# Attention and two MLPs on one core: Q and K as whole rows, V in four transfers, smaller array tiles for attention, and a planner that counts eight transfers

## The chip, the cores and the metric

The kernel runs on one core of one Trainium2 chip. The metric is the device time of one execution in microseconds (us), lower is better. Three executions of the kernel before took 1086.65, 1087.54 and 1088.17 us; their median, 1087.54 us, is its time.

## The reference

Chunked attention (chunks of 32 queries, 16 keys to the left, 8 to the right, 8 memory keys; so 64 keys for a chunk) over 4 batches, 8 heads, 768 positions and 64 dimensions, then two MLPs over the 3072 tokens that come out:

```python
for c in range(nc):                       # chunk 32, left 16, right 8, n_mem 8
    k_full = np.concatenate([mem_k, k_ctx], axis=2)
    v_full = np.concatenate([mem_v, v_ctx], axis=2)
    scores = scale * np.matmul(q_c, k_full.transpose(0, 1, 3, 2))
    scores = scores - np.max(scores, axis=-1, keepdims=True)
    a = np.exp(scores)
    a = a / (np.sum(a, axis=-1, keepdims=True) + 1e-09)
    out[:, :, c_start:c_end] = np.matmul(a, v_full)
h = x @ w_in                              # 512 -> 2048
x = (np.maximum(h, 0) + np.log1p(np.exp(-np.abs(h)))) @ w_out
h = x @ w_in2
out = (np.maximum(h, 0) + alpha * np.minimum(h, 0)) @ w_out2
```

The weights come as 64-bit floats; the kernel turns them into 32-bit ones itself.

## The kernel before

**Stages.** The 3072 tokens are six blocks of 512 (`NB`), and a block is four attention tiles of 128 queries (`TB`), so there are 24 tiles, 0 to 23. The first MLP runs in 96 steps. A step is one slice of 128 hidden units for one block: `pe_h` (12 matmuls of 128x512, tile `ps_hh`, called *h* below), softplus and a split into a high and a low part on ACT and DVE, then `pe_out` (12 matmuls, tile `ps_o`, called *o*). `SEGMENTS` (line 49) gives the order: block 0 with slices 0 to 3, block 1 with 0 to 3, block 0 with 4 to 7, block 1 with 4 to 7, and so on, so that the weights may come in while the steps run. Steps 0 to 3 need tiles 0 to 3, and steps 4 to 7, the first of block 1, need tiles 4 to 7. The second MLP (`quad`, `second`, tile `ps_q`) follows; the change leaves its arithmetic as it is.

**A tile of attention.** `load_q`, `load_k`, `load_v` fetch it. `a_mem` copies the memory keys on POOL. `a_scores` (tile `ps_s`) does Q times K on PE; `a_max` and `a_shift` or `a_bias` run on DVE, the exponential on ACT, `a_sum`, `a_norm`, `a_share` on DVE (four shares on POOL). `a_transpose` (`ps_t`) turns the result on PE, `a_turned` copies it to `pt` on ACT, `a_values` (`ps_x`) multiplies by V on PE, `a_high` on ACT and `a_low` on DVE write the split `x`.

**Loads.** All of them are issued on SP, in program order. A Q load takes only half of the row (the other half is zeros), so tiles 0 to 7 have two Q loads of 128 KB and one K load of 320 KB; from tile 8 on it is four Q loads of 64 KB and one of 320 KB. V is six transfers for every tile. Each transfer takes one of eight completion semaphores in turn, so a transfer is issued only when the eighth before it has landed.

**Weights.** A half slice of weights is one `raw` load of 512 KB and, on DVE, five operations (`magnitude`, `clamp`, `convert`: tile `word`), then a cast on ACT and a subtraction on DVE (`wsplit`). There are three `raw` rooms.

**The planner.** `Plan` (lines 87 to 182) takes pieces with an engine, an assumed length, a due time, what they wait for and what rooms they take, and writes out one order for each engine; `schedule` (line 921) states the pieces. The table `O` (line 84) shifts the due times. Where the planner sees PE idle in the first 90 us of its own time, it puts matmuls on zeros ahead of the piece (`keep_busy`, tile operand `zero`), so many as its idle time holds.

Of the kernel before, what the change touches and what calls it, by code (L numbers as in the profile page):

```python
# [16 lines left out]
P = 128  # L17
# [17 lines left out]
KEYS = (0, NMEM + CHUNK, NMEM + 2 * CHUNK, KN - KW)  # L35
BIG = 3.0e38
# [47 lines left out]
O = {'km': 86.2, 's': 61.12, 'm': -43.08, 'c': -48.65, 'e': 42.58, 'n': -133.53, 'r': -44.0, 'w': -59.36, 't': 2.28, 'pt': -87.92, 'v': 6.67, 'xh': -71.45, 'xl': 6.28, 'first': 47.53, 'gap': -183.71, 'second': 20.97, 'gap2': -27.69, 'raw': 41.75, 'ab': -85.86, 'cl': -61.09, 'ca': 10.82, 'cb': 74.39, 'cc': -95.76, 'wh': -29.12, 'wl': -22.45, 'odd': 97.94, 'sp': 116.5, 'hi': 37.44, 'lo': 2.59, 'out': 17.61, 'wait': 0.05, 'sloads': 24.5, 'km0': 68.55, 'km1': 28.97, 's0': -25.87, 's1': 2.3, 'm0': -192.19, 'm1': -112.61, 'c0': -31.95, 'c1': -25.21, 'e0': -51.53, 'e1': -16.47, 'n0': -131.79, 'n1': 72.42, 'r0': -17.47, 'r1': -5.18, 'w0': 52.91, 'w1': -43.08, 't0': -1.99, 't1': 39.24, 'pt0': -100.96, 'pt1': 70.29, 'v0': 21.52, 'v1': 14.34, 'xh0': -72.64, 'xh1': 5.24, 'xl0': 133.53, 'xl1': -30.69, 'by0': -46.78, 'by1': 30.48, 'va': -0.63, 'vb': 176.94, 'vc': -46.03, 'vd': 155.73, 'ra': -58.02, 'rb': 154.89, 'rc': 130.18, 'wld': 105.54, 'dra': -108.27, 'ca0': 58.14, 'ca1': -5.43}  # L84


class Plan:
# [18 lines left out]
    def run(self):  # L106
# [10 lines left out]
        while left:  # L117
            able, first = [], 1e9
            for name, since in ready.items():
                engine, us, due, _, _, take, _, _ = left[name]  # L120
                t = max(since, free.get(engine, 0.0) if engine else 0.0, now)
                if engine == "SP":
                    t = max(t, free.get("DMA", 0.0) - 4.0)
                for r in set(take):
                    short = take.count(r) - rooms[r]
                    if short > 0:
                        later = sorted(u for u, g in back if g == r)
                        t = max(t, later[short - 1] + self.LAG if len(later) >= short else 1e9)
                able.append((t, due, name, engine))
# [28 lines left out]
            if engine == "PE":  # L158
# [3 lines left out]
                if t < 90.0 and t - free.get("PE", 0.0) > 0.5:  # L162
                    self.idle[name] = (max(free.get("PE", 0.0), came), t)
# [14 lines left out]
            for a in then.get(name, ()):  # L178
                wants[a] -= 1
                if not wants[a]:  # L180
                    ready[a] = max(done[b] for b in left[a][4]) + self.LAG
# [4 lines left out]
def attention_mlp_mlp_kernel(ctx: ExitStack, tc, qk, v, w1, w2, consts, out):  # L186
# [15 lines left out]
    ps_a = ctx.enter_context(room_pool("ps_a", 2, bass.MemoryType.PSUM))  # L202
    early = ctx.enter_context(ExitStack())
    apool = early.enter_context(room_pool("a", 1))
# [111 lines left out]
    raw_q, q_t, k_t, v_t, st, s_room = {}, {}, {}, {}, {}, {}  # L316
    pt = [tpool.tile([P, NPAIR, 2, D], F32, tag=tag, name="pt") for tag in ("tb", "tl")]
    both = gpool.tile([P, 2, NPAIR, 2, D], F32, tag="g", name="pt2")
    pt2 = [both[:, u] for u in range(2)]

    def pt_of(t):
        return pt2 if t < TB and t % 2 else pt

    q_late = apool.tile([P, 2, 4 * NPAIR, CHUNK], F32, tag="qt", name="qt", bufs=1)

    def others(q, eng):

        for e in range(2):
            half = q[e * D:(e + 1) * D].rearrange("p c (n e) k -> p c n e k", e=2)
            for c in range(2):  # L330
                eng.memset(half[:, c, :, 1 - e], 0.0)

    def room_qk(t):
        if t < 2 * TB:
            room = wpool.tile([P, 4 * DM], F32, tag="w", name="qk0")
            raw_q[t] = room[:, :QN // 2]
            k_t[t] = room[:, QN:QN + NPAIR * KN].rearrange("p (g k) -> p g k", k=KN)
        else:
            q_t[t] = q_late
            k_t[t] = apool.tile([P, NPAIR * KN], F32, tag="kt", name="kt", bufs=1).rearrange("p (g k) -> p g k", k=KN)  # L340

    def own(q, e):

        return q[e * D:(e + 1) * D].rearrange("p c (n e) k -> p c n e k", e=2)[:, :, :, e]

    def load_q(t, e, c=None):
        part = slice(e * D, (e + 1) * D)
        rows = qk[t][part, :QN].rearrange("p (n e k) -> p n e k", e=2, k=D)[:, :, e]
        if c is None:
            sp.dma_start(out=raw_q[t][part].rearrange("p (n k) -> p n k", k=D), in_=rows)  # L350
        else:
            sp.dma_start(out=own(q_t[t], e)[:, c], in_=rows[:, :, c * CHUNK:(c + 1) * CHUNK])
# [12 lines left out]
    def load_v(t):  # L365
        for u, to, at, n in (
            (0, 0, MEM0, NMEM), (0, NMEM, 0, KW - NMEM), (0, KW, CHUNK, KW),
            (1, 0, 0, KW), (1, KW, SW - KW + NMEM, KW - NMEM), (1, 2 * KW - NMEM, MEM0 - D, NMEM),
        ):
            part = slice(u * DM, (u + 1) * DM)  # L370
            sp.dma_start(out=v_t[t][to:to + n, part], in_=v[t][at:at + n, part])

    score_ps, turned, x_ps, part_of = {}, {}, {}, {}

    def no_corners():

        for to in (pt, pt2):
            for c in range(2):
                for u in range(2):
                    dve.memset(to[u][c * D:(c + 1) * D, :, :, (1 - c) * CHUNK:(2 - c) * CHUNK], 0.0)  # L380
# [5 lines left out]

    def a_scores(t):

        ps = score_ps[t] = (ps_acc.tile([P, NPAIR, 2, KW], F32, tag="acc", name="ps_s") if t < TB
                            else ps_a.tile([P, NPAIR, 2, KW], F32, tag="pa", name="ps_s"))  # L390
        keep_busy(("s", t), ps.rearrange("p g u k -> p (g u k)"))
        if t < 2 * TB:
            q = raw_q[t].rearrange("p (n k) -> p n k", k=D)
            for g in range(NPAIR):
                for j in range(NC):
                    u, c = divmod(j, 2)
                    for e in range(2):
                        rows, at = slice(e * D, (e + 1) * D), c * D + e * CHUNK
                        pe.matmul(
                            ps[at:at + CHUNK, g, u, :], lhsT=q[rows, u * NPAIR + g, c * CHUNK:(c + 1) * CHUNK],  # L400
                            rhs=k_t[t][rows, g, KEYS[j]:KEYS[j] + KW], start=True, stop=True,
                        )
            return
        for g in range(NPAIR):
            for j in range(NC):
                u, c = divmod(j, 2)
                n = 2 * (u * NPAIR + g)
                pe.matmul(
                    ps[c * D:(c + 1) * D, g, u, :], lhsT=q_t[t][:, c, n:n + 2, :].rearrange("p e k -> p (e k)"),
                    rhs=k_t[t][:, g, KEYS[j]:KEYS[j] + KW], start=True, stop=True,  # L410
                )

    def a_max(t):

        ps, i = score_ps[t], t % TPB
        s = s_room[t][:, :SLOTS * KW] if t < 2 * TB else apool.tile([P, SLOTS * KW], F32, tag="s", name="s_sb")
        st[t] = (s.rearrange("p (g u k) -> p g u k", u=2, k=KW), s.rearrange("p (n k) -> p n k", k=KW),
                 apool.tile([P, SLOTS, 1], F32, tag="nm", name="nm", bufs=2),
                 apool.tile([P, SLOTS, 1], F32, tag="sm", name="sm", bufs=2))
        if i == 0:  # L420
            dve.memset(ps[:D, :, 0, NMEM:NMEM + LEFT], -BIG)
        if i == TPB - 1:
            dve.memset(ps[D:, :, 1, LEFT + CHUNK:LEFT + CHUNK + RIGHT], -BIG)
        dve.tensor_reduce(out=st[t][2][:, :, 0], in_=ps.rearrange("p g u k -> p (g u) k"), axis=mybir.AxisListType.X, op=ALU.max)

    def a_shift(t):
        _, s, nm, _ = st[t]
        dve.tensor_tensor(
            out=s, in0=score_ps.pop(t).rearrange("p g u k -> p (g u) k"), in1=nm.to_broadcast([P, SLOTS, KW]), op=ALU.subtract,
        )  # L430
# [5 lines left out]
    def a_shifted_exp(t):  # L436
        _, s, nm, _ = st[t]
        x = score_ps.pop(t).rearrange("p g u k -> p (g u) k")
        for n in range(SLOTS):
            act.activation(out=s[:, n, :], in_=x[:, n, :], func=AF.Exp, bias=nm[:, n, :], scale=1.0 / float(D) ** 0.5)  # L440
# [19 lines left out]
    def a_transpose(t):  # L460
        ps = turned[t] = ps_a.tile([P, NPAIR, P], F32, tag="pa", name="ps_t")
        keep_busy(("t", t), ps.rearrange("p g k -> p (g k)"))
        for g in range(NPAIR):
            pe.transpose(ps[:, g, :], st[t][0][:, g, :, :].rearrange("p u k -> p (u k)"), ident)

    def a_turned(t):

        ps = turned.pop(t)
        for u in range(2):
            for c in range(2):  # L470
                act.copy(
                    out=pt_of(t)[u][c * D:(c + 1) * D, :, :, c * CHUNK:(c + 1) * CHUNK],
                    in_=ps[u * D:(u + 1) * D, :, c * D:(c + 1) * D].rearrange("p g (e q) -> p g e q", e=2),
                )

    def a_values(t):
        src = v_t.pop(t)
        ps = x_ps[t] = (ps_h.tile([P, NPAIR, QT], F32, tag="h", name="ps_x") if t < TB
                        else ps_a.tile([P, NPAIR, QT], F32, tag="pa", name="ps_x"))
# [715 lines left out]
```

## Time and profile before

| what | value |
|---|---|
| median of three executions | 1087.54 us (1086.65 to 1088.17) |
| the profiled execution's own time | 1092.29 us |
| its span, first to last instruction | 1090.2 us |
| mean granted TensorE clock | 0.995 of full speed |
| PE busy | 1061.8 us, 97% of the span |
| DVE busy | 705.3 us, 65% |
| ACT busy | 556.9 us, 51% |
| POOL busy | 173.0 us, 16% |
| chain that ended last | PE 92%, DMA 4%, SP's queue 2%, DVE 2% |
| read from HBM, written | 154.74 MB, 46.14 MB |

Busy time is the share in which an engine worked on something, matmuls on zeros among it. The chain follows the work that ended last back to the start, and tells for each step what it waited for. Times inside an execution are counted from the first instruction.

### The profile page before, as it was taken

The numbers are of one execution on the slowest core, as the hardware profiler recorded it, in microseconds if no ns is written. First come the engines' busy times: TensorE is split into PE (matmuls) and PEld (weight loads), VectorE is DVE, ScalarE is ACT, GpSimd is POOL, SyncE is SP. The second block draws the span as 40 slices with busy tenths as digits, with TensorE's granted clock in tenths as the row PEclk, the third lists the DMA queues.
The fourth block names the chain that finished last, engine by engine and source line by source line (L and its number), as shares of the span: only waits on it lengthen the run. The fifth ranks groups of instructions, "written<-read, shape, count | busy, mean of one in ns | idle before, by whom it ended". The sixth has DMA issues, their size and how long they took to land.

```text
span 1090.2 us, 16860 instructions
## 1 busy us (share of the span) xinstructions
PE 1061.8 (97%) x6241; PEld 872.5 (80%) x6245; DVE 705.3 (65%) x1182; ACT 556.9 (51%) x988; POOL 173.0 (16%) x217
## 2 busy tenths in 40 slices
PE   5789999999999999999999999999999999999998
PEld 3568888878888888888888888888888888888886
DVE  5779978454554454464366256678766779566976
ACT  4564435455544554453244346664455755456643
POOL 1110112422322232224233400000000010000000
PEclk8999999999999999999999999999999999999999
DMA  8966674757554554554365484799875999856904
GB/s 216 203 178 190 192 188 109 180 159 178 152 156 148 167 174 125 184 156 136 106 203 189 161 300 137 274 286 323 199 284 174 322 298 261 242 217 256 373 1 77
DMA packets 173841, 214.56 MB, mean 197 GB/s; under 512 B 96064, under 2 KB 125888, under 8 KB 166848
## 3 DMA queue, kind: packets, MB, share of 16 engines
q1 hardware_dynamic: 169456, 196.59, 56.8%
q0 software_dynamic: 4032, 16.78, 8.2%
q8 instruction: 49, 0.80, 0.3%
q14 instruction: 32, 0.26, 0.1%
q10 hardware_dynamic: 272, 0.13, 0.0%
HBM read 154.74 MB, written 46.14 MB: 184 GB/s over the span
## 4 chain that ended last, share of the span: by engine, by line
PE 92%; DMA 4%; SPq 2%; DVE 2%; issue 0%; ACT 0%; POOL 0%; DVEq 0%; ACTq 0%
PE ps_q L71 42%; PE ps_hh L71 23%; PE ps_o L71 23%; SPq L71 2%; DMA raw<-in_w_dram 2%; PE ps_x L71 2%; PE ps_s L71 2%; DMA v<-in_v_dram 1%; PE ps_t L71 1%; DVE word L71 1%; DMA qk<-in_qk_dram 1%; DVE x L71 0%; DVE wsplit L71 0%; DVE g L71 0%; ACT pt L71 0%
## 5 line engine op out<-in xcount | busy, mean ns | idle before, releaser
L71 PE MATMUL ps_o<-g,wsplit 128*128 128x512 f32 x1152 | 281.2, 393 | 1.3 <-DVE g L71 1.3
L71 PE MATMUL ps_hh<-x,wsplit 128*128 128x512 f32 x1152 | 279.4, 391 | 2.9 <-ACT x L71 1.8
L71 PEld LDWEIGHTS ps_hh<-x,wsplit 128*128 128x128 f32 x1152 | 214.7, 188 | 48.6 <-ACT x L71 2.3
L71 PEld LDWEIGHTS ps_o<-g,wsplit 128*128 128x128 f32 x1152 | 215.8, 189 | 46.6 <-DVE g L71 1.6
L71 PE MATMUL ps_q<-xop,win 128*128 128x512 f32 x1008 | 229.1, 389 | 0.0
L71 PE MATMUL ps_q<-g,wout 128*128 128x512 f32 x1008 | 229.1, 389 | 0.0
L71 PEld LDWEIGHTS ps_q<-xop,win 128*128 128x128 f32 x1008 | 189.2, 188 | 39.3
L71 PEld LDWEIGHTS ps_q<-g,wout 128*128 128x128 f32 x1008 | 189.0, 188 | 39.6 <-DVE g L71 0.2
L71 DVE TENSOR_TENSOR g<-ta,g 128x512 fp32r<-128x512 f32 x96 | 70.4, 733 | 131.1 <-ACT g L71 130.6
L71 ACT CAST g<-gb 128x512 fp32r<-128x512 f32 x168 | 100.9, 622 | 91.1 <-PE ps_q L71 66.1
L71 DVE TENSOR_TENSOR g<-gb,g 128x512 fp32r<-128x512 f32 x168 | 114.2, 687 | 37.0 <-ACT g L71 35.1
L71 ACT CAST g<-ta 128x512 fp32r<-128x512 f32 x96 | 59.6, 621 | 113.9 <-PE ps_o L71 113.7
L71 ACT ACTIVATE ta<-ps_hh 128x512 f32<-128x512 f32 x96 | 57.4, 598 | 108.9 <-PE ps_hh L71 106.6
L71 DVE SCALAR_TENSOR_TENSOR word<-raw,word 128x512 int32<-128x512 int32 x128 | 93.0, 727 | 2.7
L71 ACT ACTIVATE tp<-gb 128x512 f32<-128x512 f32 x48 | 30.4, 633 | 91.5 <-DVE gb L71 91.5
L71 POOL TENSOR_TENSOR wst<-wsum,wst 128x512 fp32r<-128x512 f32 x32 | 42.8, 1338 | 146.9 <-ACT wst L71 146.9
L71 DVE TENSOR_SCALAR word<-raw 128x512 int32<-128x512 int32 x64 | 29.6, 463 | 51.2 <-DMA raw<-in_w_dram 31.7
L71 DVE SCALAR_TENSOR_TENSOR gb<-gb,tp 128x512 f32<-128x512 f32 x48 | 33.2, 692 | 44.0 <-ACT tp L71 44.0
L71 DVE TENSOR_SCALAR word<-word 128x512 f32<-128x512 f32 (+1 forms) x128 | 56.6, 447 | 1.9
L71 ACT ACT_TABLE_LOAD x38 | 48.8, 1283 | 12.0 <-DVE nm L71 11.3
L71 POOL TENSOR_TENSOR wst<-word,wst 128x512 fp32r<-128x512 f32 (+1 forms) x32 | 35.2, 1100 | 119.2 <-ACT wst L71 119.2
L71 POOL DMA_DIRECT2D gb<-gb x12 | 10.3, 862 | 262.7 <-DVE g L71 169.8
(82 smaller groups left out, 879.3 us busy)
## 6 DMA issues: line engine op xcount, KB each, us to landing
wout<-out_ops SPq DMA_DIRECT2D x42, 1024.0 KB
raw<-in_w_dram SPq DMA_DIRECT2D x64, 512.0 KB
win<-in_ops SPq DMA_DIRECT2D x24, 1024.0 KB
win<-in_ops SPq DMA_DIRECT2D x24, 768.0 KB
out_ops<-wst SPq DMA_DIRECT2D x56, 256.0 KB
in_ops<-wst SPq DMA_DIRECT2D x24, 512.0 KB
gb<-gb POOLq DMA_DIRECT2D x12, 1024.0 KB, 13.7
v<-in_v_dram SPq DMA_DIRECT2D x48, 128.0 KB
```

The lines of the kernel that those rows point to most:

```text
L71: i = getattr(self.engine, name)(*args, **kw)
```

## The change

Q and K of tiles 0 to 7 come as one transfer of whole rows, zeros included (`load_qk`, 128x1664 elements), with no memory copy for them: where the memory keys stand apart, a score matmul is split in two (`key_parts`, 8 and 56 keys). Later tiles have two Q loads and one K load. V is four transfers for each tile. Scores of every tile run on array tiles of 64 rows and 32 columns, values on 64 by 64 with half the keys and half the queries each. `pt` is one copy of 128x512 for each tile, not four of 64x256. From tile 4 on, one PSUM tile of two banks, `pair_room`, holds scores, transposes and values; tiles 0 to 3 use it for values. The planner counts eight transfers under way (`lane`), has other assumed lengths, and its table is another one.

```diff
+VROWS = (
+    (0, 56, (0, 1), (40, 1)), (56, NMEM, (56, 1), (MEM0, 0)),
+    (D + NMEM, 56, (0, 0), (40, 0)), (D, NMEM, (MEM0 - D, 1), (CHUNK, 0)),
+)
...
-                if engine == "SP":
-                    t = max(t, free.get("DMA", 0.0) - 4.0)
...
+    ps_pair = early.enter_context(room_pool("ps_pair", 1, bass.MemoryType.PSUM))
...
+    def load_qk(t):
+        sp.dma_start(out=qk_room[t][:, :QK], in_=qk[t])
...
+    def key_parts(t, j):
+
+        if t >= 2 * TB:
+            return [(0, KEYS[j], KW)]
+        if j in (1, 2):
+            return [(0, j * CHUNK, KW)]
+        n = KW - NMEM
+        return [(0, MEM0, NMEM), (NMEM, 0, n)] if j == 0 else [(0, KT - n, n), (n, MEM0, NMEM)]
...
+        for to, many, (a, u), (b, z) in VROWS[2 * h:2 * h + 2]:
+            first, step = a * 2 * DM + u * DM, (b - a) * 2 * DM + (z - u) * DM
+            sp.dma_start(
+                out=w[to:to + many],
+                in_=bass.AP(tensor=v.tensor, offset=v[t].offset + first, ap=[[2 * DM, many], [step, 2], [1, DM]]),
+            )
...
+    pair_room = ps_pair.tile([P, 2, N2], F32, tag="pair", name="ps_a")
...
+                            for to, key, many in key_parts(t, j):
+                                pe.matmul(
+                                    banks[e][at:at + CHUNK, n, 1 - u, to:to + many],
+                                    lhsT=query(t, e, u * NPAIR + g)[:, c * CHUNK:(c + 1) * CHUNK],
+                                    rhs=k[rows, g, key:key + many], start=True, stop=True,
+                                )
...
+        act.copy(out=pt[t % 2].rearrange("p (a m) k -> p a (m k)", a=2), in_=turned.pop(t))
...
+                        pe.matmul(
+                            ps[e * D:(e + 1) * D, u, g, c * CHUNK:(c + 1) * CHUNK], lhsT=src[keys, c, d0:d0 + D],
+                            rhs=pt[t % 2][keys, 2 * e + g // 2, q0:q0 + CHUNK], start=True, stop=True,
+                        )
...
+                     "acc": 4, "y": 6, "w": NF, "x": 2, "lane": 8})
...
+        def dma(name, issue, move, due, work, after=(), take=(), give=(), eng="SP", lanes=1):
+            lanes = ["lane"] * lanes if eng == "SP" else []
...
+            add(("t", t), "PE", 0.5, due - when_due("t"), lambda: a_transpose(t), [("ww", t) if few else ("w", t), ("cst",)], [tp, tb], ["s"] if few else [])
...
-            spare[name] = max(0, int((until - since - 0.5) * 0.6 / 0.22))
+            spare[name] = max(0, int((until - since - 0.2) * 0.9 / 0.22))
```

How the order moves, at three places. First SP at the start of the program (names are the destination and the source of a load; `qk_97` and `qk_98` are Q and K of tiles 0 and 1). Before, from the first load on:

```order
L71 DMA qk_97<-in_qk_dram 64x8x64
L71 DMA qk_98<-in_qk_dram 64x8x64
L71 DMA qk_97<-in_qk_dram 64x8x64
L71 DMA qk_98<-in_qk_dram 64x8x64
L71 DMA qk_97<-in_qk_dram 128x4x160
L71 DMA qk_98<-in_qk_dram 128x4x160
L71 DMA cst<-in_consts_dram 128x144
```

Now, `qk_100` and `qk_101` being tiles 0 and 1:

```order
L75 DMA qk_100<-in_qk_dram 128x1664
L75 DMA qk_101<-in_qk_dram 128x1664
L75 DMA v_106<-in_v_dram 56x2x512
L75 DMA v_106<-in_v_dram 8x2x512
L75 DMA v_109<-in_v_dram 56x2x512
L75 DMA v_109<-in_v_dram 8x2x512
L75 DMA v_109<-in_v_dram 56x2x512
L75 DMA v_109<-in_v_dram 8x2x512
L75 DMA cst<-in_consts_dram 128x144
```

Two loads stand where six stood, and V of the first tiles comes ahead of the constants.

Second PE, at the values (`ps_x`, `ps_a<-pt,v`) of the last of tiles 4 to 7, up to block 1 (x12 of `ps_hh` are one h, x12 of `ps_o` one o). Before, and behind these rows three matmuls on zeros, two h and one o:

```order
L71 MATMUL ps_x<-pt,v_521 64x64 x16
L71 MATMUL ps_hh<-x,wsplit 128x512 x12
L71 MATMUL ps_x<-pt,v_619 64x64 x16
L71 MATMUL ps_t<-cst,v_697 128x128 x4
L71 MATMUL ps_o<-g,wsplit 128x512 x12
L71 MATMUL ps_x<-pt,v_697 64x64 x16
```

Now (`ps_a` is `pair_room`):

```order
L75 MATMUL ps_a<-pt,v_639 64x32 x32
L75 MATMUL ps_hh<-x,wsplit 128x512 x12
L75 MATMUL ps_a<-pt,v_579 64x32 x32
L75 MATMUL ps_o<-g,wsplit 128x512 x12
L75 MATMUL ps_a<-cst,v_500 128x128 x4
L75 LDWEIGHTS zero
L75 MATMUL ps_hh<-zero 128x512
L75 MATMUL ps_hh<-x,wsplit 128x512 x12
L75 MATMUL ps_a<-pt,v_500 64x32 x32
L75 MATMUL ps_o<-g,wsplit 128x512 x12
L75 MATMUL ps_hh<-x,wsplit 128x512 x36
L75 MATMUL ps_o<-g,wsplit 128x512 x12
```

As many h and o stand ahead of block 1 as before (four and three), but attention there goes through one tile, and after it three h come in a row.

Third PE in the steps, around scores (`qk` or `kt`) and values (`pt,v`) of the first late tiles. Before:

```order
L71 MATMUL ps_s<-kt,qt 64x64 x16
L71 MATMUL ps_x<-pt,v 64x64 x16
L71 MATMUL ps_hh<-x,wsplit 128x512 x12
L71 MATMUL ps_o<-g,wsplit 128x512 x12
L71 MATMUL ps_hh<-x,wsplit 128x512 x12
L71 MATMUL ps_o<-g,wsplit 128x512 x12
L71 MATMUL ps_t<-cst,s_sb 128x128 x4
```

Now:

```order
L75 MATMUL ps_a<-qk 32x64 x32
L75 MATMUL ps_o<-g,wsplit 128x512 x12
L75 MATMUL ps_a<-pt,v 64x32 x32
L75 MATMUL ps_hh<-x,wsplit 128x512 x24
L75 MATMUL ps_a<-pt,v 64x32 x32
L75 MATMUL ps_hh<-x,wsplit 128x512 x12
L75 MATMUL ps_a<-cst,s_sb 128x128 x4
```

Scores and values that stood side by side stand apart here, and there are twice as many matmuls in each. Of tiles 8 to 23, 14 pairs stood together before and 4 pieces alone; now 11 pairs stand together and 10 pieces alone.

## Rows read from the trace of the kernel before

**Rows 1.** The page, busy time of each engine.

```profile
PE 1061.8 (97%) x6241; PEld 872.5 (80%) x6245; DVE 705.3 (65%) x1182; ACT 556.9 (51%) x988; POOL 173.0 (16%) x217
```

**Rows 2.** Busy time by stage: stretch, its length, then PE, PEld, DVE, ACT, POOL.

```profile
80.00:90.00 10.00, 10.00 (x46) 8.28 (x45) 9.97 (x20) 5.68 (x11) 0.00 (x0) 1.00 0.72 222
...
160.00:180.00 20.00, 20.00 (x124) 16.17 (x124) 16.16 (x31) 10.51 (x18) 2.10 (x4) 1.00 0.46 121
```

**Rows 3.** Timeline of PE, first 90 us: start, length, what.

```profile
8.13 3.23 PE L71 MATMUL ps_s<-qk 64*32 64x64 f32 x128 [3.34 <-POOL qk L71]
...
24.34 1.37 PE L71 MATMUL ps_x<-zero 128*128 128x512 bf16 x3
...
30.79 1.04 PE L71 MATMUL ps_x<-zero 128*128 128x512 bf16 x4
...
33.41 0.86 PE L71 MATMUL ps_s<-qk 64*32 64x64 f32 x45
...
49.23 1.15 PE L71 MATMUL ps_x<-pt,v 128*64 128x64 f32 x32
...
57.11 1.12 PE L71 MATMUL ps_s<-qk 64*32 64x64 f32 x64 [0.20 <-POOL qk L71]
...
77.28 5.51 PE L71 MATMUL ps_hh<-x,wsplit 128*128 128x512 f32 x23 [1.11 <-DVE x L71]
```

**Rows 4.** Waits of SP's queue, first 80 us: total, times, longest.

```profile
SPq L71 <- DVE word L71: 8.7, 3, 4.9
SPq L71 <- DMA raw<-in_w_dram: 8.3, 5, 3.4
```

**Rows 5.** Timeline of SP, first 90 us.

```profile
0.75 3.98 SPq L71 DMA_DIRECT2D qk<-in_qk_dram  x6
...
59.87 3.42 SPq L71 DMA_DIRECT2D kt<-in_qk_dram  x1
```

**Rows 6.** Timeline of DVE; in brackets the idle time before and what ended it.

```profile
10.32 0.69 DVE L71 TENSOR_REDUCE nm<-ps_s 128x8 f32<-128x512 f32 x1
...
36.03 0.69 DVE L71 TENSOR_TENSOR v<-ps_s,nm 128x512 f32<-128x512 f32 x1
...
51.13 0.68 DVE L71 TENSOR_TENSOR x<-ps_x,x 128x512 fp32r<-128x512 f32 x1
...
71.47 0.43 DVE L71 TENSOR_SCALAR word<-raw 128x512 int32<-128x512 int32 x1 [2.31 <-DMA raw<-in_w_dram]
```

**Rows 7.** Timeline of ACT, first 80 us.

```profile
46.10 1.54 ACT L71 COPY pt<-ps_t 64x256 f32<-64x256 f32 x4
```

**Rows 8.** PE and DMA by 2 us: PE busy, granted clock, DMA share, GB/s.

```profile
8.00:10.00 2.00, 1.87 (x72) 0.50 1.37 184
...
38.00:40.00 2.00, 2.00 (x10) 1.00 1.10 367
```

**Rows 9.** Timeline of PE in the steps, late tiles.

```profile
158.79 2.88 PE L71 MATMUL ps_o<-g,wsplit 128*128 128x512 f32 x12
161.60 1.15 PE L71 MATMUL ps_s<-kt,qt 128*64 128x64 f32 x32
162.69 3.02 PE L71 MATMUL ps_hh<-x,wsplit 128*128 128x512 f32 x12
165.54 2.88 PE L71 MATMUL ps_o<-g,wsplit 128*128 128x512 f32 x12
168.26 2.88 PE L71 MATMUL ps_hh<-x,wsplit 128*128 128x512 f32 x12
...
179.73 1.15 PE L71 MATMUL ps_s<-kt,qt 128*64 128x64 f32 x32
181.75 3.02 PE L71 MATMUL ps_hh<-x,wsplit 128*128 128x512 f32 x12
...
233.92 0.63 PE L71 MATMUL ps_t<-cst,s_sb 128*128 128x128 f32 x4 [2.50 <-DVE s_sb L71]
```

**Rows 10.** Timeline of DVE around the stop of PE at 231 us.

```profile
227.47 0.43 DVE L71 TENSOR_SCALAR word<-raw 128x512 int32<-128x512 int32 x1 [3.72 <-DMA raw<-in_w_dram]
```

More of the change, by code (lines that the diff above doesn't have):

```diff
@@ L180, in run @@
                 if not wants[a]:
-                    ready[a] = max(done[b] for b in left[a][4]) + self.LAG
+                    e = left[a][0]
+                    ready[a] = max(done[b] + (0.02 if e and e != "DMA" and self.pieces[b][0] == e else self.LAG) for b in left[a][4])
         self.order = order
@@ L313, in operands_at @@
         return [in_ops[q][:, :, k:k + n, :].rearrange("p a k n -> p a (k n)")]
[L316 to L331, printed above, removed]
+    raw_q, k_t, qk_room, v_t, st, s_room = {}, {}, {}, {}, {}, {}
@@ L346, in load_q @@
-    def load_q(t, e, c=None):
-        part = slice(e * D, (e + 1) * D)
[L348 to L352, printed above, removed]
+            room = qk_room[t] = wpool.tile([P, 4 * DM], F32, tag="w", name="qk0")
+            raw_q[t] = room[:, :QN].rearrange("p (n e k) -> p n e k", e=2, k=D)
@@ L470, in a_turned @@
             for c in range(2):
[L471 to L479, printed above, removed]
-        keep_busy(("v*", t), ps.rearrange("p g k -> p (g k)"))
-        for u in range(2):
-            for g in range(NPAIR):
-                for e in range(2):
-                    d0 = u * DM + (2 * g + e) * D
-                    pe.matmul(
-                        ps[e * D:(e + 1) * D, g, u * D:(u + 1) * D], lhsT=src[:, d0:d0 + D], rhs=pt_of(t)[u][:, g, e, :],
-                        start=True, stop=True,
-                    )
+                for u in range(2):
+                    for e in range(2):
+                        keys, d0, q0 = slice((1 - u) * D, (2 - u) * D), (2 * g + e) * D, (2 * c + g % 2) * CHUNK
+                        pe.matmul(
+                            ps[e * D:(e + 1) * D, u, g, c * CHUNK:(c + 1) * CHUNK], lhsT=src[keys, c, d0:d0 + D],
+                            rhs=pt[t % 2][keys, 2 * e + g // 2, q0:q0 + CHUNK], start=True, stop=True,
+                        )
@@ L595, in switch_pools @@
         late["x"] = ctx.enter_context(room_pool("y", 1))
+        late["pa"] = ctx.enter_context(room_pool("ps_a", 2, bass.MemoryType.PSUM))
     def raw_y(name):
@@ new lines, in tile @@
+            add(("vr", t), "", 0.0, soon + 2, lambda: room_v(t), [("i", "qk", t, 2)] + ([("i", "vh", prev, 1)] if few else []), vrooms)
+            for h in range(2):
+                dma(("vh", t, h), 0.95, 0.85, (O["va"], O["vb"], O["vc"], O["vd"])[t] if start else due - 24, lambda h=h: load_v(t, h),
+                    [("i", "vh", t, 0) if h else ("vr", t)], lanes=2)
+            add(("v", t), "", 0.0, 0.0, nothing, [("vh", t, h) for h in range(2)])
+            if few:
+                add(("km", t), "POOL", 0.36, due - when_due("km"), lambda: a_mem(t), [("qk", t, 2)])
@@ L1038, in tile @@
-            add(("pt", t), "ACT", 1.53, due - when_due("pt"), lambda: a_turned(t), [("t", t), "corners"], [tb], ["pa"])
+            add(("w", t), "POOL" if by_pool else "DVE", 1.06 if by_pool else 0.69, due - when_due("w"), lambda: a_share(t, pool if by_pool else dve), [("r", t)])
+            tp = "h" if start else "pa"
+            if few:
+                add(("ww", t), "", 1.5, 0.0, nothing, [("w", t)])
+            add(("t", t), "PE", 0.5, due - when_due("t"), lambda: a_transpose(t), [("ww", t) if few else ("w", t), ("cst",)], [tp, tb], ["s"] if few else [])
@@ L1040, in tile @@
+            add(("pt", t), "ACT", 0.62, due - when_due("pt"), lambda: a_turned(t), [("t", t)], [], [tp])
             free_x = [("ds", drained[t // TB - 2])] if few else []
[L1041 removed]
+            if few:
+                add(("wp", t), "", 1.0, 0.0, nothing, [("pt", t)])
+            after_v = [("wp", t) if few else ("pt", t), ("v", t)] + ([("xl", prev)] if t >= 3 * TB and t % TB == 1 else [])
+            give_x = ["pa"]
```

256 lines of the change are left out of this document (121 added, 135 removed).

## The prediction

> **What bounds the kernel now.** I read the page first. PE is busy for 1061.8 of 1090.2 us [rows 1], so all that a change can win is PE's idle time, some 28 us, the matmuls on zeros that fill other gaps, and the length of PE's own pieces. The stages show where the idle time lies: from 80 us on PE is busy throughout, while DVE, at 9.97 of 10 us, has just enough time for the weights; it gets air only later, 16.16 of 20 us [rows 2]. So the span is two things: the moment at which the first h of block 1 starts, 77.28 us [rows 3], and what PE has to do from there.
>
> Before that moment the timeline of DVE is the one to read. It begins with the maximum of tile 0 at 10.32 us and stands still several times for a late weight load, the last time for 2.31 us [rows 6]. These loads are late because SP issues in order: the six loads of Q and K at the start take SP 3.98 us, one K load of tile 8 held SP for 3.42 us until an earlier transfer had landed [rows 5], and SP waits 8.7 us for rooms and 8.3 us for weight loads that hold its semaphores [rows 4].
>
> From there on the timeline of PE in the steps gives prices. A plain piece takes 2.72 us (165.54 to 168.26). Scores alone take 1.09 us to the next start, and the two neighbours lose 0.09 and 0.13 us: 1.31 us. Scores and values together take 2.02 us, with the same edges 2.24 us. And PE stops once, for 2.50 us before the transposes at 233.92 us [rows 9]; the cause is a weight load that DVE had waited 3.72 us for, ahead of the softmax in its queue [rows 10].
>
> **Loads at the start, removed and added.** Two transfers instead of six must land for tiles 0 and 1, and POOL's copy of the memory keys is gone from the chain. But tile 0 now needs 0.85 MB, not 0.59 MB. Narrow Q rows moved at 184 GB/s, wider ones at 367 GB/s [rows 8]; at the second rate 0.85 MB is 2.3 us. I put the scores of tile 0 at 6 us in place of 8.13 us [rows 3]. Bounds: 5 us if the rate is reached at once, 8.5 us at the lower rate.
>
> **Scores of tiles 0 to 7.** Splitting makes 96 instructions out of 64 in the trace (a matmul in 32-bit floats shows as two), over the same number of columns. 64 take 1.12 us, 17.5 ns each [rows 3]. By columns a tile stays at 1.12 us, by instructions it is 1.68 us; I take 1.4 us. At the start PE ran at half its clock (granted 0.50, that is 1.2 GHz) [rows 8], and 128 instructions took 3.23 us [rows 3], 25 ns each: 2.4 us for tile 0. So DVE starts some 1.9 us earlier than before.
>
> **The one PSUM tile.** This is the new wait. Values of tiles 0 to 3 and everything of tiles 4 to 7 take turns in it, and the next piece waits until DVE has read it out. From values on: 1.15 us on PE at 49.23 us, and the subtraction on DVE ends at 51.81 us [rows 3, 6], 2.6 us a turn. From scores: 1.4 us, then two DVE operations of 0.69 us [rows 6] and the handovers, 2.9 us. From transposes: 0.63 us [rows 9] and one copy, 0.6 us if it costs what a DVE operation of that size does, since four copies of half a tile took 1.54 us [rows 7]: 1.35 us. Zeros in PE's order come on top when their turn is late: 0.26 us each, 0.46 us at the lower clock (1.04 us for four, 1.37 us for three) [rows 3].
>
> Tiles 0 to 3: four turns and 22 matmuls on zeros behind tile 3's scores, of which I count two thirds as seen, put the scores of tile 4 at 35 us, where they stood at 33.41 us [rows 3]. So the early start is spent here. Tiles 4 to 7: four turns of scores, 11.6 us, with three plain pieces between them that outlast DVE by 1.3 us each, 3.9 us: 50.5 us. Then four turns of transposes, 5.4 us, four of values, 10.4 us, 15 zeros, 3.9 us, and four plain pieces that hold PE when the tile is free, 4.5 us: 74.7 us. The first h of block 1 follows a piece o and starts near **75.2 us, 2.1 us earlier**. What SP waited for no longer counts: with five issues for a tile in place of nine the loads of weights stand ahead of their use, and the tile takes their place as the bound. Bounds: 70 us if the zeros hide and the scores take 1.12 us, 82 us if zeros and scores run at the lower clock.
>
> **Late tiles, more pieces alone.** Before there are 4 pieces alone and 14 pairs, 4 x 1.31 + 14 x 2.24 = 36.6 us [rows 9]. Now there are 10 and 11: 37.7 us. That is **+1.1 us**. The 16 transposes stay what they were.
>
> **Late tiles, smaller array tiles.** Scores have 64 instructions in place of 32; 64 of that form take 1.12 us in the early tiles [rows 3] and the 32 take 1.15 us [rows 9]. They go over eight parts of the array in turn where the early ones used four, so they may gain more. Values have no row: 64 instructions of half the columns. Nearest is again the early scores, 1.12 us against 1.15 us. I take 0.03 us for each and 0.03 us for the eight parts, **-1.0 us** over 16 tiles. Bounds: each halves, -18 us; each instruction for values costs what one does now, 36 ns [rows 3], +18 us.
>
> A cost for each instruction is in fact what one page says. The Trainium skill, "TensorEngine Tiling (Array Packing)", section "Instruction Overhead", has some 60 cycles for every matmul and warns not to tile a dimension that is already small; at 2.4 GHz an estimate from it is 25 ns, and 64 instructions would take 1.6 us. The 17.5 ns of [rows 3] stand against that, for instructions that go to different parts of the array.
>
> **The stop at 233 us.** V is four issues in place of six, late Q two in place of four, and the planner now counts the eight transfers. I expect the load in [rows 10] in time: **-2.5 us**. Now h and o come in runs of two to four, each of which needs its rooms freed in time by ACT and DVE; for such stops I add **+0.5 us** (nothing to 4 us).
>
> **Nothing.** The second MLP has the same work on PE. The zeroing on DVE and POOL that goes was over before the first scores.
>
> **Sum.** -2.1 + 1.1 - 1.0 - 2.5 + 0.5 = -4.0 us. The profiled execution took 1092.29 us; it would take 1088.3 us. It stands 4.75 us above the median of 1087.54 us, and so I predict **1083.5 us**.
>
> **Rivals.** *The one tile decides the start.* For it speaks that 67 matmuls on zeros stand in PE's new order where 29 stood, and that each tile now hands it over three times. If zeros and scores run at the lower clock, block 1 starts at 82 us, 6.8 us later than forecast: 1090.3 us, slower than before. It turns at a start of about 79 us, where the whole change comes to nothing. Against it: DVE has spare time there, so it may read out at once. 18%.
>
> *Each small matmul has its own price.* At 25 ns values take 1.6 us, 0.45 us more than now, 7.2 us over 16 tiles, and the 0.5 us that I took as gained for them is lost: 1083.5 + 7.7 = 1091.2 us. That is the lower clock's price in [rows 3], where the clock explains it; at full clock 17.5 ns speak against it. 7%. The page named above is the one that would have it so.
>
> *It wins more.* The eight parts work at once, 0.25 us less for scores of 16 tiles, -4 us, and block 1 starts at 71 us: 1083.5 - 8 = 1075 us. DVE, which has little spare time from 80 us on [rows 2], speaks against more than that. 15%.
>
> *The loads were not the bound.* The change lightens them, and neither the start nor the stop moves: 1083.5 + 2.1 + 2.5 = 1088.1 us, no change. The waits of [rows 4] and [rows 10] speak against it. 5%.
>
> **How the numbers follow.** The forecast keeps 55%, from 1080 to 1087 us. Within 0.2%, 2.2 us, is what a measurement of this kernel can't tell from no change: 1085.4 to 1089.7 us. Of the forecast's 55, 45 lie below that and 10 within; of the first rival 14 are slower and 4 within; the second is slower; the third faster; the fourth within, with one point slower. That gives 0.60, 0.18 and 0.22. For 8 times in 10 the range goes from 1074 us, which holds most of the third, to 1091 us, which holds the first and half of the second; the outer bounds of the small tiles lie beyond it and are left out.
>
> **What would show it.** Right: scores of tile 0 at about 6 us, of tile 4 near 35 us, the first h of block 1 after seven plain pieces near 75 us; before it, SP no longer waiting for weight loads and DVE waiting for PE and ACT in place of DMA; scores and values of a late tile in 2.0 us; no stop above 1 us after 200 us. Wrong: block 1 after 79 us, values above 1.3 us, or new stops in the runs of o. If it starts before 71 us, the turns of the one tile were priced too high.

## The result and the profile after

The changed kernel takes 1101.02 us (four runs, 1098.08 to 1103.45) against 1087.1 us before (the median with a fourth run, 1084.79 us): ratio 1.013, 95% interval 1.0096 to 1.0163. It is slower by some 14 us; the forecast was 1083.5 us. The profiled execution took 1098.08 us, span 1096.3 us, and is the fastest of the four. (In the experiments one execution of the second run, 1699.93 us, and the profiled one of the third, 1544.5 us, ran at granted clocks of 0.59 and 0.65 and enter no ratio.)

PE's line of the page, to be held against [rows 1]: its busy time has *grown* by 11 us, in 1578 more matmuls.

```profile
PE 1072.7 (98%) x7819; PEld 874.7 (80%) x7819; DVE 709.2 (65%) x1179; ACT 537.3 (49%) x916; POOL 167.9 (15%) x197
...
q8 instruction: 61, 1.00, 0.4%
```

The second line is the DMA queue that brings instructions: packets, MB, share. It matters below.

Timeline of PE of the changed kernel, start and length, in brackets the idle time before and what ended it:

```profile
5.53 1.69 PE L75 MATMUL ps_s<-qk 64*32 64x8 f32 x96 [2.21 <-DMA qk<-in_qk_dram]
...
17.89 1.69 PE L75 MATMUL ps_s<-qk 64*32 64x8 f32 x96 [3.04 <-DMA qk<-in_qk_dram]
...
24.23 1.15 PE L75 MATMUL ps_s<-qk 64*32 64x8 f32 x87 [0.50 <-DMA qk<-in_qk_dram]
28.88 0.48 PE L75 MATMUL ps_s<-qk 64*32 64x8 f32 x9 [3.50 <-issue]
29.29 1.93 PE L75 MATMUL ps_a<-pt,v 64*64 64x32 f32 x64
31.15 1.11 PE L75 MATMUL ps_t<-cst,v 128*128 128x128 f32 x4
32.65 3.22 PE L75 MATMUL ps_a<-zero 128*128 128x512 bf16 x10 [0.39 <-DVE x L75]
35.80 1.14 PE L75 MATMUL ps_a<-pt,v 64*64 64x32 f32 x64
...
43.72 1.25 PE L75 MATMUL ps_a<-qk 64*32 64x8 f32 x96
...
86.89 8.32 PE L75 MATMUL ps_hh<-x,wsplit 128*128 128x512 f32 x36
...
263.13 1.14 PE L75 MATMUL ps_a<-pt,v 64*64 64x32 f32 x64
264.19 0.86 PE L75 MATMUL ps_a<-qk 64*32 64x64 f32 x64
264.98 5.75 PE L75 MATMUL ps_o<-g,wsplit 128*128 128x512 f32 x24
```

Block 1 starts at 86.89 us, where [rows 3] had 77.28 and the forecast 75.2. From there to the end it is 1009.4 us, against 1012.9. So the whole loss lies in the first 87 us. Tile 0 is early, as forecast. Then three things are to be seen. Tiles 2 and 3 wait for their Q and K. Inside tile 3's scores PE stands still for 3.50 us with nothing to wait for ("issue"); with two shorter ones such stops take 4.6 us up to block 1. And then come the turns of `pair_room`, of which the chain of waits shows one whole (start, length, what):

```profile
29.36 1.90 PE ps_a L75 x64
31.26 0.02 issue
31.29 0.59 ACT x L75
31.88 0.02 issue
31.90 0.70 DVE x L75
32.61 0.04 issue
32.65 4.33 PE ps_a L75 x74
```

Values, ACT's copy, DVE's subtraction, and the next PE piece, which begins with ten matmuls on zeros. They write the tile themselves, so they can't fill the wait for it: they begin when it is over. From 29 to 72 us the zeros ahead of such pieces take 3.22, 1.25, 1.68, 1.46, 2.72 and 0.59 us, 10.9 us, all on this chain.

### The profile page after: what moved, and what is told of

Same layout as the page of the kernel before. It is cut to its first block, busy times and chain, and to the rows that moved or that the text cites. A ratio compares the mean times of both kernels' runs of the same rounds, so it can differ in the third digit from the quotient of the medians.

```text
span 1096.3 us, 19695 instructions
## 1 busy us (share of the span) xinstructions
PE 1072.7 (98%) x7819; PEld 874.7 (80%) x7819; DVE 709.2 (65%) x1179; ACT 537.3 (49%) x916; POOL 167.9 (15%) x197
## 4 chain that ended last, share of the span: by engine, by line
PE 96%; DMA 2%; issue 1%; DVE 0%; ACT 0%; SPq 0%; ACTq 0%
PE ps_q L75 42%; PE ps_o L75 24%; PE ps_hh L75 24%; PE ps_a L75 6%; DMA qk<-in_qk_dram 1%; DMA v<-in_v_dram 1%; SPq L75 0%; DVE x L75 0%; ACT x L75 0%; ACT pt L75 0%; PE ps_s L75 0%; DVE v L75 0%; DVE nm L75 0%; DVE c L75 0%; DVE o_sb L75 0%
## 5 line engine op out<-in xcount | busy, mean ns | idle before, releaser
L75 PE MATMUL ps_o<-g,wsplit 128*128 128x512 f32 x1152 | 276.6, 392 | 0.0
L75 PE MATMUL ps_hh<-x,wsplit 128*128 128x512 f32 x1152 | 275.2, 391 | 0.0
L75 DVE TENSOR_SCALAR word<-word 128x512 f32<-128x512 f32 (+1 forms) x128 | 58.9, 460 | 4.0
```

Of the source, the lines that this page charges most:

```text
L75: i = getattr(self.engine, name)(*args, **kw)
```

## The experiments

Four theories. **A**: the loads of tiles 2 and 3 are late. **B**: PE's stops "issue", in which its next instructions are not there yet. **C**: the turns of the one tile with the zeros in them. **D**: the zeros as such. All ratios are to the kernel before; the change has 1.013.

**Loads and zeros.** First run: Q's own halves and K as three loads. Second: Q and K of tiles 2 and 3 issued ahead of V. Third: both. Fourth: fewer zeros.

```diff
-        sp.dma_start(out=qk_room[t][:, :QK], in_=qk[t])
+        rows = qk[t][:, :QN].rearrange("p (n e k) -> p n e k", e=2, k=D)
+        for e in range(2):
+            part = slice(e * D, (e + 1) * D)
+            sp.dma_start(out=raw_q[t][part, :, e], in_=rows[part, :, e])
+        sp.dma_start(out=qk_room[t][:, QN:QK], in_=qk[t][:, QN:])
...
-    for piece in plan.order:
...
+    for piece in rest[:at] + sooner + rest[at:]:
...
-            spare[name] = max(0, int((until - since - 0.2) * 0.9 / 0.22))
+            spare[name] = max(0, int((until - since - 0.5) * 0.6 / 0.22))
```

> Q and K of an early tile come as three transfers again: the tile's own halves of Q (twice 64 rows) and K. The zeros between them stay behind (0.59 MB a tile in place of 0.85 MB); the room's layout and the order of every other piece are the change's. Theory A, the bytes of the whole rows: at some 300 GB/s the 0.79 MB saved up to the scores of tile 2 bring them from 17.89 us to near 15.5 us, those of tile 3 from 24.23 us to near 21 us, and the first h of block 1 from 86.89 us to near 84 us; the time falls by some 3 us against the change. Theory B, PE's own stops for instructions: the stop of 3.5 us in tile 3's scores stays and the start of block 1 moves by under 1 us. Theory C, the one PSUM tile: scores of tiles 2 and 3 come earlier, those of tile 4 stay near 43.7 us and block 1 near 87 us.

> SP issues Q and K of tiles 2 and 3 right behind those of tiles 0 and 1, ahead of the V loads of tiles 0 and 1; every other instruction stays in its order. Theory A, order of the loads: scores of tile 2 near 11 us (now 17.89), of tile 3 near 14 us (now 24.23); V of tile 0 lands some 5 us later and its values wait instead; in all block 1 starts 3 to 6 us earlier than 86.89 us and the time falls by as much. Theory B, PE's stops: scores come earlier, but a stop of some 3 us appears elsewhere in the first 48-wide runs, and block 1 gains under 2 us. Theory C, the one PSUM tile: the gain before tile 3 is lost again in the turns, block 1 within 1 us of 86.89 us.

> Both of these together: own halves of Q and K alone, and Q and K of four tiles ahead of V. Theory A: the two gains add up, block 1 at some 79 to 82 us and the time 5 to 8 us below the change. Theory B: under 2 us. Theory C: no more than 1 us, since what is late is the turn of the tile and not its operands.

> Only the number of matmuls on zeros in the gaps is set as before (0.6 of a gap less 0.5 us, in place of 0.9 of a gap less 0.2 us): some 30 fewer. Theory D, the zeros delay what follows them: 30 matmuls at 0.26 to 0.46 us are 8 to 14 us of PE time, of which a third is on the path, so block 1 starts 3 to 4 us earlier. Theory A: they stand in gaps that wait for loads, and the start moves by under 1 us in either direction, or is later if the clock falls to 0.50 for longer.

Measured: 1.0114 [1.0097, 1.0132], 1.0140 [1.0123, 1.0157], 1.0150 [1.0133, 1.0167] and 1.0110 [1.0082, 1.0138]: none wins anything clear. A as a cause by itself falls. With fewer bytes tile 3's scores begin only 0.7 us earlier. With Q and K ahead of V those of tile 2 are ready but stand in PE's order behind a transpose that now waits 2.85 us for the constants, and PE stops twice for over 1 us. Timeline of PE of the second run:

```profile
16.05 0.94 PE L75 MATMUL ps_t<-cst,v 128*128 128x128 f32 x4 [2.85 <-DMA cst<-in_consts_dram]
...
23.99 1.28 PE L75 MATMUL ps_a<-pt,v 64*64 64x32 f32 x36 [2.51 <-issue]
...
30.73 0.48 PE L75 MATMUL ps_s<-qk 64*32 64x8 f32 x9 [1.71 <-issue]
```

So in the first two runs the gain at the loads met stops of B, as that theory had said: 7.2 and 6.5 us of them in all, 4.6 in the change.

**The zeros inside the turns, and the turns.** Fifth run: the same zeros, written to a bank that nobody waits for. Sixth: left out. Seventh: as the fifth, and values of tiles 1 and 2 in the other half of the tile.

```diff
+        if name[1] >= TB or name[0] == "v*":
+            ps = None if not n else acc[0][0] if add else first_banks[2 if name == ("v*", 1) else 0]
...
+        for _ in range(0 if name[1] >= TB or name[0] == "v*" else n):
...
-        room = pair_room[:, :, HK:]
+        room = pair_room[:, :, HK:] if t >= TB or t in (0, 3) else pair_room[:, :, :HK]
```

> The same number of matmuls on zeros in the same places, but those ahead of values, transposes and scores that write the one PSUM tile go to a bank that nobody waits for (up to tile 4's scores an early score bank; later a bank of the sums, to which zero is added), so they run while DVE still reads the tile. Theory C, the turns of the one tile with zeros inside them: in the change the chain from 29 to 72 us is values, ACT's copy, DVE's subtraction, zeros, next piece, again and again, with 10.9 us of zeros. Beside the reading, they cost only what outlasts it: values of tile 2 gain 1 us, of tile 3 1.2, scores of tile 4 1.4, the three transposes 1.3, 2.5 and 0.6; block 1 starts at 79 to 80 us in place of 86.89 and the time falls by 6 to 9 us. Theory B (PE's stops for instructions) and the loads: the same waits come back elsewhere, under 2 us.

> Those matmuls on zeros are left out (36 of them, 10.9 us), those in the banks of the early scores stay. Theory C: all of it is on the path, block 1 starts at 75 to 77 us and the time falls by 10 to 12 us, unless PE's granted clock stays at 0.50 in the gaps, which at twice the length for all plain pieces up to there would give half of it back. Theory B and the loads: under 2 us.

> As the run with the zeros put aside, and values of tiles 1 and 2 write the half of the tile that tile 4's scores take later, so that values of tile 2 need not wait for tile 1's result to be read. Theory C: one turn of some 2.0 us (copy and subtraction) falls out of the chain, of which the ten zeros ahead of values 2 fill the larger part: 0 to 2 us earlier than the zeros aside alone. If the number of zeros and not the turn now sets the time: no difference.

Measured: 1.0081 [1.0066, 1.0096], 1.0111 [1.0094, 1.0129] and 1.0073 [1.0058, 1.0088]. Zeros put aside win some 5 us (the intervals of the fifth run and of the change just touch), less than the 6 to 9 us expected. So C holds for the zeros inside the turns; for the turns by themselves it is not shown, since the second half of the tile adds nothing that can be told. In the fifth run's profile block 1 starts at 84.19 us, 2.7 us earlier than in the change, and its stops grew to 7.9 us. A stop can cost more than its length. Timeline of PE of the fifth run, at tile 4's scores:

```profile
43.49 1.45 PE L75 MATMUL ps_a<-qk 64*32 64x64 f32 x76 [3.25 <-issue]
44.88 5.08 PE L75 MATMUL ps_hh<-x,wsplit 128*128 128x512 f32 x12
```

This h, behind the stop, ran at a granted clock of 0.50 (from 44 to 48 us) and took 5.08 us, where the same h takes 3.01 us in the change.

Left out, the zeros win 2 us at most, since PE then runs at 1.2 GHz for longer. Stretches of the sixth run, then of the change (PE, PEld, DVE, ACT, POOL busy, granted clock, DMA share, GB/s):

```profile
30.00:50.00 20.00, 15.02 (x355) 12.70 (x356) 15.57 (x32) 7.77 (x18) 0.51 (x1) 0.57 0.83 262
```

```profile
30.00:50.00 20.00, 17.34 (x414) 11.98 (x410) 15.72 (x33) 8.89 (x20) 0.97 (x1) 0.89 0.89 271
```

In the sixth run the first h takes 4.23 us, in the change 3.01. So the zeros are worth having (D falls; 1.0081 with them aside, 1.0111 without) and stand in the wrong bank. And where a turn got shorter, PE's stops grew: 12.2 us of them in the seventh run, 4.6 in the change. Timeline of PE of the seventh:

```profile
22.50 1.28 PE L75 MATMUL ps_a<-pt,v 64*64 64x32 f32 x36 [4.35 <-issue]
...
30.34 0.34 PE L75 MATMUL ps_s<-qk 64*32 64x8 f32 x9 [2.81 <-issue]
...
38.85 0.59 PE L75 MATMUL ps_a<-pt,v 64*64 64x32 f32 x26 [2.02 <-issue]
```

**Fewer instructions.** Eighth run: early scores as 64 instructions, POOL copying the memory keys as before, Q as whole rows and K apart. Ninth: this and the zeros aside. Tenth and eleventh: these, the second half, and Q and K of tile 2 (tenth) or of tiles 2 and 3 with the constants (eleventh) ahead of V.

```diff
-        n = KW - NMEM
-        return [(0, MEM0, NMEM), (NMEM, 0, n)] if j == 0 else [(0, KT - n, n), (n, MEM0, NMEM)]
+        return [(0, KEYS[j], KW)]
...
+        if t < 2 * TB:
+            a_mem(t)
```

> Early scores as 64 instructions in place of 96: the memory keys are copied by POOL again to both ends of each group of keys; Q still comes as whole rows in one transfer, K in a second one with a gap in its rows; the zeros stay where the change has them. Theory B, PE's instructions: a third fewer instructions in the early scores, 1.25 us a tile becomes 0.9 us and the stop of 3.5 us goes or halves: block 1 2 to 5 us earlier. Theory C: scores are beside the turns for tiles 0 to 3, and 0.3 us for each of tiles 4 to 7: 1 us earlier, with the copy on POOL ahead of each score given back.

> The 64-instruction scores and the zeros put aside, in one kernel. Theories B and C are both true and independent: the start loses both PE's stops (4.6 us in the change's trace) and the zeros inside the turns (some 7 us): first h of block 1 near 76 us, the time 1084 to 1086 us, that is, 13 to 16 us below the change and level with the kernel before or just under it. If the two are the same time seen twice (a stop fills a turn): no better than the 64-instruction scores alone, block 1 at 80 to 81 us and 1089 us or more. If the loads are the next bound: scores of tile 3 stay at 26 us and block 1 comes at 78 to 80 us.

> As the run before it, values of tiles 1 and 2 in the other half of the one tile, and Q and K of tile 2 ahead of the V loads. Loads as the next bound: scores of tile 2 come from 17.6 us to near 13 us, those of tile 3 stay, since what is moved ahead is only in its place, and the gain is under 1 us. If the order of the loads matters as such: 1 to 3 us.

> As the run before it, with Q and K of tile 3 and the constants ahead of the V loads too. Loads as the next bound: scores of tile 3 come from 26 us to 15 to 18 us; V of tile 1 lands at some 20 us and values start there; everything up to tile 4 moves 3 to 5 us up, if V comes in time, and block 1 starts at 72 to 74 us, 1081 to 1083 us. If V is then the late one: scores of tile 4 stay where the run with only tile 2's Q and K ahead has them.

Measured: 1.0096 [1.0059, 1.0134], 1.0038 [1.0019, 1.0056], 1.0038 [1.0021, 1.0055] and 1.0022 [1.0007, 1.0038]. Alone, fewer instructions seem to win some 4 us, but the eighth run's interval overlaps that of the change: its four executions spread over 10 us, and the profiled one is the fastest. On top of the zeros put aside they win 5 us, which is clear (1.0081 to 1.0038). Both together win 10 us, more than either alone, if less than the 13 to 16 us expected: so they are separate causes. Not all of what fewer instructions win is stops, since a tile's scores now take 0.86 us in place of 1.25. In the eighth run's profile block 1 starts at 80.90 us, 6.0 us earlier than in the change: stops fell from 4.6 to 0.7 us, and shorter scores of tiles 4 to 7 give 1.6 us. The ninth's profile has 7.6 us of stops again, so fewer instructions make stops rarer, not impossible. With the loads in order as well, a step that is not clear by itself, most of the 14 us is given back; timeline of PE of the eleventh run, block 1:

```profile
76.88 8.32 PE L75 MATMUL ps_hh<-x,wsplit 128*128 128x512 f32 x36
```

**What a stop is.** The page counts 7819 matmuls and as many weight loads, 15638 instructions, which came in 61 packets: 256 in each, 128 matmuls with their weight loads. In the profiles of the change and of runs 1 to 11 without the third, the stops of over 0.35 us in the first 100 us, but for two of 0.35 and 0.37 us, stand 125 to 128 weight loads apart or a multiple of that: in the first run behind the 348th, 475th, 602nd, 728th, 855th and 982nd matmul, in the change behind the 477th, 984th and 1111th. That is the end of a packet. The trace also has the packets themselves. DMA queues of the change (packets, MB, share): from 24 to 26 us only loads move; from 26 to 28 us one packet of instructions is among them:

```profile
q1 hardware_dynamic: 193, 0.45, 107.0%
```

```profile
q8 instruction: 1, 0.02, 4.5%
```

PE ran out at 25.38 us; the packet's transfer began at 26.04 us and took 1.43 us, and PE went on 1.4 us later, at 28.88 us. In the same way each of the 37 stops of these profiles ends 1.2 to 1.8 us after a packet has landed. So B is shown: PE waits for instructions.

A stop needs a fast run through the packet before. In the first run PE took 3.0 us for the 128 matmuls up to the stop in tile 3's scores and stood for 3.3; in the seventh 3.1 and 4.4; in the change 3.6 and 3.5. Where PE took 7.5 us or more, because it waited for something else, it never stood for over 0.5 us, but for one stop of 0.7 and one of 0.9. But the pace doesn't set the length: another 3.2 us in the first run were followed by a stop of 0.5 us, and 6.1 us in the fifth by one of 3.3. From the time that PE enters a packet before a stop until the next is there it takes some 4 to 10 us during the loads; the transfer itself is 0.9 to 1.6 us of it. In the kernel before PE took some 7 to 15 us for each packet, and stops sum up to 0.2 and 0.8 us in two profiles.

**The kernel before again, and cut.** Twelfth run: before, unchanged. Fourteenth: before with its early pieces cut into as many instructions as the change has.

```diff
+                        cut = {0: NMEM, 3: KW - NMEM}.get(j, KW)
+                        for k0, k1 in ((0, cut), (cut, KW)):
...
+                    parts = ((0, D),) if t >= 2 * TB else ((0, CHUNK), (CHUNK, D))
```

> The kernel before, unchanged, profiled a second time. In its first profile block 1 starts at 77.28 us, and 1012.9 us follow up to the end; in the change and the runs derived from it 1008.5 to 1009.4 us follow. Theory L, the late tiles gain by their form: again some 1010 to 1013 us after the start of block 1. Theory M, the first profile held a stray stop (2.5 us at 233 us) and the change won nothing there: 1009 us or less.

> The kernel before with the early scores cut into 96 instructions in place of 64 and the early values into 64 in place of 32, over the same columns; loads, order, zeros and the late tiles are those of before. Theory B, PE's instructions arrive too late while the loads run: stops of PE with nothing to wait for, 0.8 us before, grow to 3 to 8 us up to 77 us, and the time rises by 2 to 6 us. Theory C alone (the one PSUM tile): the two are as fast as before, 8 tiles by some 0.1 to 0.2 us.

The second profile of before took 1086.23 us: block 1 starts at 73.91 us and 1010.2 us follow, without a stop; in it PE goes on where [rows 9] showed 2.50 us of waiting. So that stop was a stray one, as theory M has it; but 1010.2 us lies within what theory L named, not M, and the late tiles keep a gain of some 1 us. Before cut takes 1.0044 [1.0029, 1.0059], 5 us more, but with a single stop of 1.3 us: its time went into the values, 2.08 us for a tile in place of 1.15. Timelines of PE, of the cut kernel, then of the second profile of before:

```profile
22.27 2.08 PE L71 MATMUL ps_x<-pt,v 128*64 128x32 f32 x64
...
79.38 5.49 PE L71 MATMUL ps_hh<-x,wsplit 128*128 128x512 f32 x23 [0.22 <-DVE x L71]
```

```profile
62.84 1.15 PE L71 MATMUL ps_x<-pt,v 128*64 128x64 f32 x32
...
73.91 5.51 PE L71 MATMUL ps_hh<-x,wsplit 128*128 128x512 f32 x23 [0.23 <-DVE x L71]
...
227.89 0.60 PE L71 MATMUL ps_t<-cst,s_sb 128*128 128x128 f32 x4
```

So B as it was put there, by the number of instructions alone, missed: PE went through the cut packets in some 4 to 9 us up to 67 us and stood once.

**One part at a time.** Fifteenth run: before, with Q of tiles 0 to 7 as whole rows. Sixteenth: before with the change in the late tiles alone (the thirteenth was a first form of it, in which a transpose could overwrite a result not yet read; it showed 1.0006 [0.9995, 1.0016]). Seventeenth: the change with its early loads cut small.

```diff
+            if e == 0:
+                sp.dma_start(out=raw_q[t], in_=qk[t][:, :QN])
...
+        if t >= 2 * TB:
+            src = src.rearrange("p (c n) -> p c n", c=2)
+            ps = x_ps[t] = pair_room[:, :, HK:].rearrange("p u (g k) -> p u g k", k=D)
...
+            for c in range(2):
+                sp.dma_start(
+                    out=w[to:to + many, c],
```

> The kernel before, with Q of tiles 0 to 7 as whole rows in one transfer of 512 KB in place of two of 128 KB; K, V, order, instructions and zeros as before. Theory Q, large transfers under way: PE's instructions come through the same DMA engines and wait behind the transfers under way, so stops of PE with nothing to wait for appear (3 us or more up to 77 us, 0 to 0.9 us in the three runs of before's order), and the start of block 1 comes later: 2 to 5 us slower. If the transfers' size does nothing to PE's stops: stops under 1 us, and the start within 2 us of before.

> Late tiles as in the change, the early ones, the planner's rules and the table as before, now with each transpose behind the reading of the previous tile's result and with the halves of the one PSUM tile given out as they come free. From the runs so far 1010.2 us follow the start of block 1 in the kernel before and 1008.2 to 1009.4 us with late tiles of the new form: 1 to 2 us less than before, 1084.5 to 1086 us, if the early part is left as it was. If the turns of the one tile cost the early part something: no gain, 1086 to 1089 us.

> The change with its early loads cut small: Q's own halves and K as three transfers (128, 128 and 320 KB), V of every tile in eight of at most 112 KB; order, instructions and zeros are the change's. Theory Q: with less under way at a time PE's stops fall from 4.6 to 7.2 us to under 2 us and the time by some 3 us; more issues on SP may take a part of it back. If the stops come from the number of PE's instructions alone: 4 us or more of stops, and no gain.

Measured: 0.9987 [0.9977, 0.9996], 1.0017 [1.0007, 1.0027] and 1.0101 [1.0087, 1.0115]. The fifteenth, 1085.51 us, is the fastest kernel here: whole rows of Q are a small gain by themselves, 1.4 us with an interval that just leaves out 1, and the one part of the change that showed a gain alone. Its timeline of PE:

```profile
7.33 3.06 PE L71 MATMUL ps_s<-qk 64*32 64x64 f32 x128 [2.21 <-POOL qk L71]
...
71.60 7.12 PE L71 MATMUL ps_hh<-x,wsplit 128*128 128x512 f32 x23 [1.11 <-DVE x L71]
```

Large transfers bring no stops there (0.5 us), though PE takes 7 us or more for a packet there as in before, which may hide them. Small ones don't take the stops from the change (6.6 us in the seventeenth), and there theory Q falls. The late tiles alone win nothing in all. After block 1, 1009.7 us follow, half a microsecond less than in the second profile of before, although PE stops three times after 200 us, 1.5 us in all. The early pieces wait more: 5.6 us for DVE's softmax ahead of pieces in the one tile, where the second profile of before has 1.1.

## Why the prediction was wrong

*Loads at the start.* Scores of tile 0 at 6 us: measured 5.53. Right, and DVE's first maximum came 2.9 us earlier than in [rows 6]. But the step stopped at tile 1. Tiles 2 and 3 have no term: their Q and K land at 17.86 and 24.19 us, 10 and 11.7 us after their issue, behind V.

*Scores of tiles 0 to 7.* Forecast 1.4 us, measured 1.25 at full clock and 1.69 at the lower one (tile 2).

*The one PSUM tile.* The walk put tile 4's scores at 35 us; they came at 43.72. Of the walk the turns and zeros came out right in sum, by luck: from tile 3's scores to tile 4's it counted four turns and two thirds of the zeros, 14.2 us; measured were 14.4 us, but three turns with all 22 zeros, 6.2 us, at the lower clock in part. What failed is the sentence "What SP waited for no longer counts" and the silence on PE's own instructions: tile 3's scores ended at 29.36 us, where 35 less 14.2 leaves 20.8. That is 8.6 of the 11.7 us by which block 1 missed 75.2 us: 3.5 the stop, 5.1 the late load of tile 3, as far as the chain of waits tells. SP's wait had only moved: up to 80 us it waits 18.8 us for Q, K and V to land, 5.5 before. Waits of SP's queue in the change, then before, and the load of tile 3 in the chain of waits (start, length, what):

```profile
SPq L75 <- DMA qk<-in_qk_dram: 12.6, 8, 5.0
SPq L75 <- DMA v<-in_v_dram: 6.2, 9, 1.1
```

```profile
SPq L71 <- DMA qk<-in_qk_dram: 4.9, 5, 2.0
...
SPq L71 <- DMA v<-in_v_dram: 0.6, 2, 0.4
```

```profile
12.47 11.72 DMA qk<-in_qk_dram
```

The other 3 us lie between tile 4 and block 1: the 15 zeros took 5.2 us, not 3.9, in part at the lower clock, and stops 1.1 us. And the zeros need not have been on the path: in another bank they cost some 5 us less (fifth run).

*The stop at 233 us, -2.5 us.* It was a cost of that one execution: the second profile of before lacks it. And the prediction used it twice, once as a gain and once more inside the 4.75 us by which it moved its sum down to the median. The first profile's start was late too, 77.28 against 73.91 us.

*Late tiles.* More pieces alone +1.1, small array tiles -1.0, new stops +0.5: from block 1 on, +0.6 us once the stray stop is set aside. To measure it, both have to be counted alike: 77.28 and 73.91 us are the second matmul of the first h, whose first stands 1.6 and 0.7 us ahead, and 86.89 us is the first. From the second matmul on 1009.2 us follow in the change and 1010.2 in the second profile of before, -1.0 us; runs 1 to 11 (without the third) and 17 have 1008.3 to 1009.1. So the late tiles gained 1 to 2 us where the sum had a loss. Values and scores side by side take 1.85 us to the next start where [rows 9] had 2.02, the scores in it 0.79 us where scores alone had 1.09; the values take 1.14 us in 64 instructions, 1.15 in 32. So the rival with a price for each small matmul fell: 64 take 1.06 us to the next start, not 1.6.

*Rivals.* "The one tile decides the start" had the right sign and the nearest start (block 1 at 82 us), and was given 18%; its 1090.3 us is still 11 us short. Its zeros are shown, worth 5 us, but its condition, "if zeros and scores run at the lower clock", held in part only: they cost because they write the bank that they wait for. The rest of the loss, PE running out of instructions and the late loads of tiles 2 and 3, was in no rival, though for the first [rows 1] and the order gave the number of instructions.

SP, as forecast, waits less for weight loads (3.3 us against 8.3 in [rows 4]), and DVE waits for PE: both without use to the time.

## What to carry to other kernels

Filler work must not write the buffer whose release it bridges; put it where nobody waits, and keep it, since the clock falls without it. Count the instructions that a run of small matmuls takes from the instruction stream, and ask how many microseconds one packet of them lasts while the DMA engines are full (here a busy share of 0.9 to 1.1 from 4 to 36 us); a piece that takes no longer in twice the instructions can be dearer there. And take a second profile of the kernel before, before a stop in the first one is booked as a gain.

## What the hardware showed beside this

PE's instructions come in packets of 16.4 KB, 256 at a time, and during the loads the next was there some 4 to 10 us after PE had entered the last. The transfer took 0.9 to 1.6 us, and PE went on 1.2 to 1.8 us behind it; why it begins so late was not settled. Small loads (run 17) don't end the stops, and the number of instructions (run 14) doesn't bring them alone.

The form of a small matmul decides its price: 64 instructions for values over 64x64 parts of the array take 1.14 us, 17.8 ns each; 64 of the same 32 columns over 128x64 parts take 2.08 us, 32.5 ns each (run 14), hardly less than the 36 ns of those with 64 columns (32 of them in 1.15 us, before). The Trainium skill, "TensorEngine Tiling (Array Packing)", section "Instruction Overhead", has some 60 cycles for every matmul, by an estimate 25 ns at 2.4 GHz; the two forms lie on either side of it.
